# A second weight load moved from the head of a decode kernel to its tail, with two column tiles, and one copy per engine and one semaphore for the output

## The chip, the cores and the metric

The kernel runs on one core of a Trainium2 chip. The metric is the device time of one execution in microseconds. All executions told here were of the fast state; their granted TensorE clock (the share of full speed that the matmul engine was given, 0.50 or 1.00 at any moment), averaged over the span, was 0.775 to 0.789. Each execution has a time and, a little shorter, the span of the profile. The difference is what comes before the first and after the last recorded work; it was 1.76 to 1.94 us in 27 executions of the kernel before.

## The reference, cut to what matters

One decode step for two sequences. Branch A is attention of 16 query heads over a cache of 8 x 32768 keys and values per sequence, and a projection WO (4096 x 448). Branch B is a small MLP, W1 (448 x 1792), GELU, W2 (1792 x 448). A sigmoid gate mixes the two.

```python
g = _sigmoid((x * gate_w).sum(-1, keepdims=True))
a = _A_ref(x, A_k_cache, A_v_cache, A_wq, A_wo)      # softmax(q K^T) V, then @ wo
b = _B_ref(x, B_w1, B_b1, B_w2, B_b2)                # gelu(x @ w1 + b1) @ w2 + b2
return g * a + (1 - g) * b
```

The two caches make 536.9 MB of the 547.4 MB read. W2 is 1.6 MB, WO 3.7 MB.

## The kernel before

One queue loads everything through a ring of three slots of 8.4 MB: WQ, W1 and W2 share the first slot, then come the tiles of K and V, and last WO, in four pieces. The parts that the change touches (cuts marked):

```python
WOP = (0, 14, 26, 30, 32)            # WO's pieces, in chunks of 128 rows
DQ = Dm // 4                         # 112 columns: four column tiles
...
order = [("WQ", 0), ("W12", 0)]      # W1 and W2 together
# ... K and V tiles ...
order += [("V", LASTV), ("WO", 0)]
...
def do_FB():                         # second product of branch B, at the head
    ...
    for fc in range(FC):             # 14 x 4 matmuls, 128x2 stationary, 112 columns moving
        for q in range(4):
            e.matmul(ps_a[32 * q:32 * q + Bn, :], hT_bf[:, fc, :], w2_v[:, fc, q * DQ:(q + 1) * DQ], ...)
...
def FIN(i):                          # projection with WO, piece i: 32 x 4 matmuls in all
    E.wait(f"pW{i}", ("wo", i))
    for c in range(WOP[i], WOP[i + 1]):
        for q in range(4):
            e.matmul(ps_a[32 * q:32 * q + Bn, :], attnT[:, c:Bn * NC:NC], wo_v[...], ...)
...
# PE, at the end: PV of the last V tile, OT (fold over partitions), TT (transpose), FIN
# ACT: two copies of 112 columns to out_sb;  DVE: two more
# SP:
E.wait("dve", "mix")
E.wait("act", "mix")
dma(lambda e: e.dma_start(out[:, 0, :], out_sb), "d_out", "out")
```

FB and FIN add into the same sums in PSUM (`ps_a`), so nothing else joins the branches. Four outputs at partitions 0, 32, 64 and 96 are four column tiles of the PE array, which run at the same time: FIN took 24.7 ns for each matmul of 112 columns, where a score matmul of 512 columns over the whole array took 427 ns at the same half clock, that is 93 ns for 112 columns.

Names used below: PE, DVE, ACT and SP are the matmul, vector, scalar and synchronising engines. S are the score matmuls (q K^T), PV the product of the probabilities with V, HT the first product of branch B (with W1). A transfer has landed when its last semaphore increment has come. The trace calls `ps_a` and `out_sb` by the memory that they lie in, ps_f and pexp.

## Time and profile before

| | kernel before |
|---|---|
| time, median of 4 beside the changed kernel | 1274.07 us (1273.90 to 1274.15) |
| span of the profile | 1272.2 us |
| bytes read | 547.43 MB |
| last piece of V landed | 1259.90 us |
| WO's last piece landed | 1268.53 us |
| FIN ended | 1268.98 us |
| output issued / second landing of the output | 1269.96 / 1271.79 us |

From the page of the kernel before: the busy time of PE, the busy share of the DMA engines in 40 slices of the span (9 is 90% or more), the mean rate, and the chain of work that ended last.

```profile
span 1272.2 us, 8282 instructions
...
PE 693.5 (55%) x4640; PEld 145.3 (11%) x2112; DVE 686.0 (54%) x529; ACT 43.8 (3%) x184; POOL 3.3 (0%) x14
...
DMA  9999999999999999999999999999999999999998
...
HBM read 547.43 MB, written 0.00 MB: 430 GB/s over the span
...
DMA 63%; DVE 20%; PE 14%; issue 3%; SPq 0%; another core or an unknown queue 0%; DVEq 0%
```

The DMA engines are busy for 90% or more of every slice but the last. The Trainium skill, "DMA: Bandwidth & Descriptors", section Specifications, gives 435 GB/s as the ceiling of the fabric; this trace's 430 GB/s agrees. The kernel is bound by its bytes, so a change that removes none can only touch what lies before the stream starts and after it ends.

The end of the timeline (start, duration, engine, line, operation, count, and in brackets how long the engine had been idle and what released it):

```profile
1259.94 1.89 PE L536 MATMUL ps_o<-ring,PT 128*24 128x512 bf16 x16 [3.85 <-DMA ring<-in_A_v_cache_dram]
...
1265.54 0.22 DVE L789 CAST attnT<-ps_m 128x64 bf16<-128x64 f32 x1 [0.77 <-PE ps_m L559]
...
1265.82 3.16 PE L548 MATMUL ps_f<-ring,attnT 128*2 128x112 bf16 x128 [0.32 <-DVE attnT L789]
1269.03 0.50 ACT L653 CAST pexp<-ps_f 2x112 bf16<-2x112 f32 x2 [41.61 <-PE ps_f L548]
1269.03 0.54 DVE L792 CAST pexp<-ps_f 2x112 bf16<-2x112 f32 x2 [3.27 <-PE ps_f L548]
1269.96 0.34 SPq L395 DMA_DIRECT2D out_dram<-pexp  x1
```

Read it as one chain: the last piece of V, its product, the folds on DVE, OT, normalisation, TT, the copy of attnT, and FIN, which runs without a gap from 1265.82 to 1268.98. Then two copies on each of two engines, and the output.

The same stretch by windows (columns: window, its length, busy us and count for PE, weight loads, DVE, ACT, POOL, then the granted PE clock, DMA share and GB/s):

```profile
core 0: us, PE busy (x) PEld busy (x) DVE busy (x) ACT busy (x) POOL busy (x), PEclk, DMA share, GB/s
...
1260.00:1262.00 2.00, 1.84 (x16) 0.38 (x16) 0.11 (x1) 0.00 (x0) 0.00 (x0) 0.50 1.01 427
...
1264.00:1266.00 2.00, 0.78 (x29) 0.69 (x32) 0.91 (x3) 0.00 (x0) 0.00 (x0) 0.50 0.95 389
1266.00:1267.00 1.00, 1.00 (x56) 1.00 (x49) 0.00 (x0) 0.00 (x0) 0.00 (x0) 0.50 0.73 290
1267.00:1268.00 1.00, 1.00 (x56) 1.00 (x48) 0.00 (x0) 0.00 (x0) 0.00 (x0) 0.50 0.42 151
1268.00:1269.00 1.00, 0.97 (x44) 0.66 (x32) 0.00 (x0) 0.00 (x0) 0.00 (x0) 0.50 0.01 2
```

The clock is 0.50 through all of FIN, and the stream is nearly empty from 1268 on (2 GB/s).

At the head (timeline), FB is hidden: it takes 1.48 us, and the first transpose of K comes 10 us later.

```profile
29.92 1.48 PE L455 MATMUL ps_f<-ring,hT_bf 128*2 128x112 bf16 x56 [1.78 <-DVE hT_bf L713]
...
40.20 6.70 DVE L720 STREAM_TRANSPOSE ring<-ring 128x2048 uint32<-128x2048 uint32 x3 [10.33 <-DMA ring<-in_A_k_cache_dram]
```

### The profile page before, as it was taken

To read this page: it belongs to the slowest core of one execution; us is meant where nothing else is said; L and a number is where in the kernel's file an instruction comes from. 1 tells how busy PE (TensorE), PEld (TensorE's weight loads), DVE (VectorE), ACT (ScalarE), POOL (GpSimd) and SP (SyncE) were. 2 spreads that over 40 slices of the span, in tenths; PEclk is the share of its full clock that TensorE was granted. 3 is DMA by queue.
4 is the path that set the end of the run, shared out by engine and by line. 5 is a ranking of instruction groups with operands and counts; after the bars stand their busy time and mean duration, and the time that the engine had idled before them with its cause. 6 is when DMAs were issued, how large, how long until landed. Compare 5 with 4: busy or idle time off the path is not lost.

```text
span 1272.2 us, 8282 instructions
## 1 busy us (share of the span) xinstructions
PE 693.5 (55%) x4640; PEld 145.3 (11%) x2112; DVE 686.0 (54%) x529; ACT 43.8 (3%) x184; POOL 3.3 (0%) x14
## 2 busy tenths in 40 slices
PE   4566566545566444765445655445664546654465
PEld 3111111100111000111001111001110001110011
DVE  2675546745376553655635567353665536556351
ACT  1000000000000000000000000000000000000000
POOL 1000000000000000000000000000000000000000
PEclk9978887777887677877778877788877788867786
DMA  9999999999999999999999999999999999999998
GB/s 409 429 433 429 437 441 427 433 427 441 431 437 435 429 431 433 439 431 437 435 429 431 439 433 431 439 433 429 431 441 431 435 437 431 431 433 439 431 423 353
DMA packets 10973, 547.62 MB, mean 430 GB/s; under 512 B 1352, under 2 KB 1616, under 8 KB 1872
## 3 DMA queue, kind: packets, MB, share of 16 engines
q1 hardware_dynamic: 10804, 547.43, 99.6%
q8 instruction: 9, 0.15, 0.0%
q14 instruction: 4, 0.03, 0.0%
q10 hardware_dynamic: 156, 0.01, 0.0%
HBM read 547.43 MB, written 0.00 MB: 430 GB/s over the span
## 4 chain that ended last, share of the span: by engine, by line
DMA 63%; DVE 20%; PE 14%; issue 3%; SPq 0%; another core or an unknown queue 0%; DVEq 0%
DMA ring<-in_A_k_cache_dram 60%; DVE ring L720 18%; PE ps_s L487 4%; PE ps_s L334 4%; PE ps_o L334 3%; DMA ring<-in_A_v_cache_dram 3%; DVE mx L724 1%; PE ps_o L536 1%; PE ps_m L496 0%; PE ps_m L501 0%; DVE gmax L726 0%; PE ps_f L548 0%; DVE gmx L730 0%; SPq L376 0%
## 5 line engine op out<-in xcount | busy, mean ns | idle before, releaser
L720 DVE STREAM_TRANSPOSE ring<-ring 128x2048 uint32<-128x2048 uint32 x256 | 565.2, 2274 | 393.0 <-DMA ring<-in_A_k_cache_dram 392.8
L487 PE MATMUL ps_s<-ring,Abd 128*128 128x512 bf16 x1024 | 426.1, 416 | 429.8 <-DVE ring L720 429.4
L334 PE MATMUL ps_s<-ring,Abd 128*128 128x512 bf16 x1024 | 422.8, 413 | 0.0
L487 PEld LDWEIGHTS ps_s<-ring,Abd 128*128 128x128 bf16 x1024 | 106.0, 104 | 851.5 <-DVE ring L720 483.5
L334 PE MATMUL ps_o<-ring,PT 128*24 128x512 bf16 x1504 | 111.9, 404 | 0.0
L536 PE MATMUL ps_o<-ring,PT 128*24 128x512 bf16 x544 | 57.1, 418 | 12.8 <-DMA ring<-in_A_v_cache_dram 12.8
L506 PE MATMUL ps_f<-o_sb,selg 128*32 128x257 f32 x32 | 17.0, 636 | 83.4 <-DVE o_sb L761 83.4
L761 DVE SCALAR_TENSOR_TENSOR o_sb<-ps_o,mask,o_sb 128x256 f32<-128x256 f32 x112 | 54.2, 484 | 9.1 <-PE ps_o L536 5.1
L724 DVE TENSOR_REDUCE mx<-ps_s 128x1 f32<-128x1024 f32 x16 | 19.6, 1225 | 60.0 <-PE ps_s L334 60.0
L632 ACT ACTIVATE negm<-ps_m 128x1 f32<-128x1 f32 x16 | 2.7, 171 | 1157.6 <-PE ps_m L501 1157.6
L737 DVE STREAM_TRANSPOSE PT<-pexp 128x1024 bf16<-128x1024 bf16 x16 | 19.9, 1244 | 36.8 <-PE ps_o L334 36.8
L536 PEld LDWEIGHTS ps_o<-ring,PT 128*24 128x24 bf16 x544 | 14.6, 98 | 102.3 <-issue 85.3
L734 DVE COPY ls<-lsum 128x1 f32<-128x1 f32 x16 | 2.5, 154 | 31.8 <-ACT pexp L636 31.8
L626 ACT COPY Abd<-qrep 32x16 bf16 (+1 forms) x128 | 19.4, 199 | 0.6
L636 ACT ACTIVATE pexp<-ps_s,negm 128x1024 bf16<-128x1024 f32 x16 | 17.8, 1113 | 1.7
L496 PE MATMUL ps_m<-ident_f,mx 128*1 128x128 f32 x32 | 6.1, 270 | 21.1 <-DVE mx L724 21.1
L758 DVE TENSOR_SCALAR o_sb<-ps_o,mask 128x256 f32<-128x256 f32 x16 | 7.6, 475 | 15.7 <-PE ps_o L334 15.7
L506 PEld LDWEIGHTS ps_f<-o_sb,selg 128*32 128x32 f32 x32 | 2.9, 141 | 101.5 <-DVE o_sb L761 101.5
L501 PE MATMUL ps_m<-ones_f,gmx 1*128 1x1 f32 x32 | 6.0, 256 | 9.9 <-DVE gmx L730 9.9
L726 DVE TENSOR_REDUCE gmax<-ps_m 1x2 f32<-1x128 f32 x16 | 4.5, 278 | 7.5 <-PE ps_m L496 7.5
L419 PE MATMUL ps_s<-xT,ring 128*128 128x2 bf16 x128 | 3.6, 165 | 8.2 <-DMA ring<-in_A_wq_dram 8.2
L501 PEld LDWEIGHTS ps_m<-ones_f,gmx 1*128 1x128 f32 x32 | 4.7, 183 | 14.6 <-DVE gmx L730 14.6
(76 smaller groups left out, 61.5 us busy)
## 6 DMA issues: line engine op xcount, KB each, us to landing
ring<-in_A_v_cache_dram SPq DMA_DIRECT2D x1, 4096.0 KB, 26.8
ring<-in_A_v_cache_dram SPq DMA_DIRECT2D x2, 2048.0 KB, 33.5
ring<-in_A_wq_dram SPq DMA_DIRECT2D x1, 3072.0 KB, 10.6
ring<-in_B_w_dram SPq DMA_DIRECT2D x1, 1568.0 KB, 17.9
ring<-in_A_wo_dram SPq DMA_DIRECT2D x1, 1568.0 KB, 32.4
ring<-in_B_w_dram SPq DMA_DIRECT2D x1, 1344.0 KB, 13.7
ring<-in_A_wo_dram SPq DMA_DIRECT2D x1, 1344.0 KB, 35.3
ring<-in_A_wq_dram SPq DMA_DIRECT2D x1, 512.0 KB, 11.4
```

Of the source, the lines that this page charges most:

```text
L334: return e.add_instruction(mybir.InstMatmult(name=f"I-{nc.next_id()}", engine=mybir.EngineType.PE, ldweights=False, ins=[e.lower_ap(x), e. ...
L487: fn = lambda e, o=o, x=x, st=st, sp=sp, s=s, w=w: e.matmul(o, a_win(s, w), x, start=st, stop=sp, skip_group_check=True)
L501: E.ins(lambda e: e.matmul(ps_m[:, C_BC:C_BC + 1], gmx[:, :], ones_f[0:1, 0:1], start=True, stop=True), key=("M2", g))
L506: E.ins(lambda e: e.matmul(ps_oa, selg[:, :], o_sb[:, :], start=False, stop=False, skip_group_check=True), key=("OT", g))
L536: fn = lambda e, o=o, x=x, wt=wt, st=st, sp=sp, j=j: e.matmul(o, wt, x, start=st, stop=sp, skip_group_check=True)
L626: E.ins(lambda e, o=o, Q=Q, c=c: e.copy(o[:, :, c:c + 2], qrep[32 * Q:32 * Q + 32, :, bass.ds(E.dyn(2 * g, 2), 2)]), key=(("A", g) if (Q = ...
L636: E.ins(lambda e: e.activation(pexp[:, :].rearrange("p (r i a) -> p i r a", r=CR, i=2), ps_s[:, :].rearrange("p (i r a) -> p i r a", i=2, ...
L720: E.ins(lambda e: e.transpose(k_words(idx, blk), k_words(idx, blk)), key=("T", idx, blk))
L724: E.ins(lambda e: e.tensor_reduce(mx[:, :], ps_s[:, :], AX.X, ALU.max), key=("MX", g))
L737: E.ins(lambda e: e.transpose(PT[:, :], pexp[:, :]), key=("PT", g))
L758: E.ins(lambda e, p=p, m=m: e.tensor_scalar(o_sb[:, 0:Dh], p, m, None, op0=ALU.mult), key=("OS0", g))
L761: E.ins(lambda e, p=p, m=m: e.scalar_tensor_tensor(out=o_sb[:, 0:Dh], in0=p, scalar=m, in1=o_sb[:, 0:Dh], op0=ALU.mult, op1=ALU.add), key= ...
```

## The change

Intent: take W2 out of the head, so that K, V and the chain behind the last V piece come earlier by W2's transfer, and fill the PE's idle time in the tail with FB. Halve the number of matmuls in FB and FIN by two tiles of 224 columns. Shorten the last step to one copy on each of two engines and a single semaphore. WO's four pieces also become 16, 12, 3 and 1 chunks instead of 14, 12, 4 and 2, and the product with b2 stays at the head. The core of the diff:

```diff
-    WOP = (0, 14, 26, 30, 32)
-    DQ = Dm // 4
+    WOP = (0, 16, 28, 31, 32)
+    DQ = Dm // 2
...
-        order = [("WQ", 0), ("W12", 0)]
+        order = [("WQ", 0), ("W1", 0)]
...
-        order += [("V", LASTV), ("WO", 0)]
+        order += [("V", LASTV), ("W2", 0), ("WO", 0)]
...
-            E.wait("dve", "mix")
-            E.wait("act", "mix")
+            E.wait_total("mix")
...
-                    for q in range(4):
+                    for q in range(2):
                         E.ins(lambda e, c=c, q=q: e.matmul(
-                            ps_a[32 * q:32 * q + Bn, :], attnT[:, c:Bn * NC:NC],
+                            ps_a[64 * q:64 * q + Bn, :], attnT[:, c:Bn * NC:NC],
... (the same in FB and in the product with b2)
             OT(NG - 1)
             TT()
+            do_FB()
             E.wait("dve", "at")
...
-            for q in (2, 3):
-                E.ins(lambda e, q=q: e.copy(out_sb[:, q * DQ:(q + 1) * DQ], ps_a[32 * q:32 * q + Bn, :]),
-                      key=("mix" if q == 3 else None))
+            E.ins(lambda e: e.copy(out_sb[:, DQ:Dm], ps_a[64:64 + Bn, :]), key="mixa", stream="mix")
... (the same on DVE with tensor_copy)
```

More of the change, by code (lines that the diff above doesn't have):

```diff
@@ L190, in bass_gated_mix__gqa_block_cached__dense_activation_gelu__decode_kernel @@
         sch.stream(nm, 1)
+    sch.stream("mix", 1)
     for i in range(NB):
@@ L196, in bass_gated_mix__gqa_block_cached__dense_activation_gelu__decode_kernel @@
         sch.stream(f"pW{i}", 16)
-    for nm in ("d_w12", "d_x", "d_gw", "d_b", "d_out"):
+    for nm in ("d_w1", "d_w2", "d_x", "d_gw", "d_b", "d_out"):
         sch.stream(nm, 16)
@@ L269, in kv_src @@
             return cache[b, kvh, t * P * R:(t + 1) * P * R, :].rearrange("(p r) d -> p (r d)", p=P)
-        W_WQ, W_W12 = KC * HD + HW, KC * Fd + HF + FC * Dm
-        assert W_WQ + W_W12 <= SLOT
+        W_WQ, W_W1 = KC * HD + HW, KC * Fd + HF
+        assert W_WQ + W_W1 <= SLOT and (NC + FC) * Dm <= SLOT
         LASTV = NTILES - 1
-        order = [("WQ", 0), ("W12", 0)]
+        order = [("WQ", 0), ("W1", 0)]
         for i in range(NTILES + LAG):
@@ L279, in bass_gated_mix__gqa_block_cached__dense_activation_gelu__decode_kernel @@
                 order.append(("V", i - LAG))
-        order += [("V", LASTV), ("WO", 0)]
-        slot_of = {("WQ", 0): 0, ("W12", 0): 0}
+        order += [("V", LASTV), ("W2", 0), ("WO", 0)]
+        slot_of = {("WQ", 0): 0, ("W1", 0): 0}
         rot = [d for d in order if d[0] in "KV" and d != ("V", LASTV)]
@@ L285, in bass_gated_mix__gqa_block_cached__dense_activation_gelu__decode_kernel @@
         s_wo = slot_of[("V", LASTV - 2)]
-        slot_of[("WO", 0)] = s_wo
+        slot_of[("WO", 0)] = slot_of[("W2", 0)] = s_wo
         slot_of[("V", LASTV)] = slot_of[("K", NTILES - 1)]
@@ L291, in bass_gated_mix__gqa_block_cached__dense_activation_gelu__decode_kernel @@
             s = slot_of[d]
-            if d == ("W12", 0):
+            if d in (("W1", 0), ("WO", 0)):
                 before_of[d] = []
@@ L303, in released @@
             kind, idx = d
-            return {"K": ("S", idx, NCK // 2 - 1), "V": ("PV", idx), "WQ": "QT", "W12": "FB"}[kind]
+            return {"K": ("S", idx, NCK // 2 - 1), "V": ("PV", idx), "WQ": "QT", "W1": "HT"}[kind]
         cut = lambda s, lo, n: ring[:, s * SLOT + lo:s * SLOT + lo + n]
@@ L310, in bass_gated_mix__gqa_block_cached__dense_activation_gelu__decode_kernel @@
         w1_v = w1_f.rearrange("p (k n) -> p k n", k=KC)
-        w2_f = cut(0, W_WQ + KC * Fd + HF, FC * Dm)
+        w2_f = cut(s_wo, NC * Dm, FC * Dm)
         w2_v = w2_f.rearrange("p (f n) -> p f n", f=FC)
@@ L370, in prog_sp @@
                         dma(lambda e, o=o, src=src: e.dma_start(o, src), "slot0", ("wq", i))
-                elif kind == "W12":
+                elif kind == "W1":
                     parts = [(w1_f, B_w1[0:KC * P, :].rearrange("(p k) n -> p (k n)", p=P)),
-                             (w1_r, B_w1[KC * P:Dm, :].rearrange("p (h n) -> (p h) n", h=2)),
-                             (w2_f, B_w2.rearrange("(p f) n -> p (f n)", p=P))]
+                             (w1_r, B_w1[KC * P:Dm, :].rearrange("p (h n) -> (p h) n", h=2))]
                     for i, (o, src) in enumerate(parts):
-                        dma(lambda e, o=o, src=src: e.dma_start(o, src), "d_w12", ("w12", i))
+                        dma(lambda e, o=o, src=src: e.dma_start(o, src), "d_w1", ("w1", i))
+                elif kind == "W2":
+                    dma(lambda e: e.dma_start(w2_f, B_w2.rearrange("(p f) n -> p (f n)", p=P)), "d_w2", "w2")
                 elif kind == "WO":
@@ L433, in do_HT @@
             def do_HT():
-                E.wait_total("d_w12")
+                E.wait_total("d_w1")
                 E.wait("dve", "omB")
@@ L445, in do_HT, with do_B2 @@
                             key=("HT" if (fc == FC - 1 and hf == 1) else None))
+            def do_B2():
+                E.wait("dve", "b2f")
+                for q in range(2):
+                    E.ins(lambda e, q=q: e.matmul(ps_a[64 * q:64 * q + Bn, :], dg[:, :], b2_f[:, q * DQ:(q + 1) * DQ],
+                                                  start=False, stop=False, skip_group_check=True))
             def do_FB():
-                E.wait("dve", "b2f")
-                for q in range(4):
-                    E.ins(lambda e, q=q: e.matmul(ps_a[32 * q:32 * q + Bn, :], dg[:, :], b2_f[:, q * DQ:(q + 1) * DQ],
-                                                  start=False, stop=False, skip_group_check=True))
                 E.wait("dve", "hT")
+                E.wait_total("d_w2")
                 for fc in range(FC):
-                    for q in range(4):
+                    for q in range(2):
                         E.ins(lambda e, fc=fc, q=q: e.matmul(
-                            ps_a[32 * q:32 * q + Bn, :], hT_bf[:, fc, :], w2_v[:, fc, q * DQ:(q + 1) * DQ],
-                            start=False, stop=False, skip_group_check=True),
-                            key=("FB" if (fc == FC - 1 and q == 3) else None))
+                            ps_a[64 * q:64 * q + Bn, :], hT_bf[:, fc, :], w2_v[:, fc, q * DQ:(q + 1) * DQ],
+                            start=False, stop=False, skip_group_check=True))
             def do_GG():
@@ L546, in FIN @@
                 for c in range(WOP[i], WOP[i + 1]):
-                    for q in range(4):
+                    for q in range(2):
                         E.ins(lambda e, c=c, q=q: e.matmul(
-                            ps_a[32 * q:32 * q + Bn, :], attnT[:, c:Bn * NC:NC],
+                            ps_a[64 * q:64 * q + Bn, :], attnT[:, c:Bn * NC:NC],
                             wo_v[:, c * Dm + q * DQ:c * Dm + (q + 1) * DQ], start=False, stop=(c == NC - 1),
-                            skip_group_check=True), key=("FIN" if (c == NC - 1 and q == 3) else None))
+                            skip_group_check=True), key=("FIN" if (c == NC - 1 and q == 1) else None))
             def TT():
-                E.wait("pool", "ts1")
                 E.wait("dve", "on")
@@ L566, in prog_pe @@
             do_HT()
-            do_FB()
+            do_B2()
             def K(idx):
@@ L587, in prog_pe @@
             PV(LASTV)
+            E.wait("pool", "ts1")
             OT(NG - 1)
             TT()
+            do_FB()
             E.wait("dve", "at")
@@ L790, in prog_dve @@
             E.wait("pe", "FIN")
-            for q in (0, 1):
-                E.ins(lambda e, q=q: e.tensor_copy(out_sb[:, q * DQ:(q + 1) * DQ], ps_a[32 * q:32 * q + Bn, :]),
-                      key=("mix" if q == 1 else None))
+            E.ins(lambda e: e.tensor_copy(out_sb[:, 0:DQ], ps_a[0:Bn, :]), key="mixd", stream="mix")
         progs = {"pool": prog_pool, "sp": prog_sp, "pe": prog_pe, "act": prog_act, "dve": prog_dve}
```

## The prediction

> **What bounds the kernel now.** The page shows 547.4 MB read in a 1272.2 us span, 430 GB/s, with the DMA engines at 9 tenths in every slice but the last; the chain of waits is 63% DMA, PE and DVE are busy 55% and 54%. The Trainium skill, "DMA: Bandwidth & Descriptors" (Specifications), gives a fabric ceiling of 435 GB/s; this trace agrees. The change moves no byte out of the kernel, so only the head and the tail can move.
>
> **Tail before (timeline from 1256 us).** Last V piece 1259.94; last PV 1.9 us; the two DVE folds, OT, normalise, TT and the attnT copy follow; FIN (128 matmuls of 112 columns) runs 1265.82 to 1268.98 without a gap, 24.7 ns each; copies 0.54 us; then the output DMA. The table of stretches shows the DMA nearly empty from 1268.0. So the end is bound by the compute chain behind the last V piece, with WO landing about 1 us ahead of FIN's end.
>
> **What moves.** W2 (1.6 MB) at 425 GB/s is 3.75 us (estimate). K0, and with it every tile to the last V piece, lands 3.75 us earlier: last V piece at about 1256.2, TT done about 1261.8. The stream's end stays at about 1268.0. W2 lands at about 1260, before TT ends, so FB does not wait for it. FB (before: 56 matmuls, 1.48 us at 29.9 us, hidden under the wait for K0) is now in the tail.
>
> **Two column tiles.** PV shows four column tiles overlapping: in the cold state 12 matmuls of 512 columns take about 1.3 us net, 107 ns each, a quarter of the 427 ns pitch of the full-array score matmuls. The clock in the tail before is 0.50 from 1256.7 on. 224 columns at half clock are about 187 ns, over two tiles 93 ns a matmul, against 4 x 112 columns at 23.3 (measured 24.7). So at half clock FB costs 28 x 93 = 2.6 us and FIN 64 x 93 = 6.0 us instead of 3.16: half the instructions, twice the streaming time. Warm, 1.3 and 3.0 us.
>
> **Sum (estimate).** FB 1261.8 to 1264.4, when WO's first piece (16 of 32) lands, 1264.2. If the clock stays at half, FIN ends at about 1270.4, 1.4 us later than before. If continuous work releases it (Trainium skill, "TensorE: Matmul & The Clock Gate", Part 1: about 3.4 us of sustained work; PV here went warm 2.6 to 3.1 us after its bursts began at 1240.4 and 1250.2), FIN follows WO's landings and ends 1268.4 to 1269.1. I am not sure that this thin work counts: 6.7 us of dense two-column HT matmuls at the head did not warm it (the score matmuls at 44.8 us are still cold). One copy of 224 columns in place of two of 112 saves about 0.16 us on each of ACT and DVE; the single semaphore little. Weighted: +0.4 minus 0.2, about +0.2 us. I predict 1274.3 us, 1273.0 to 1275.6; faster by over 2%: 0.005, within 2%: 0.985, slower: 0.01.
>
> **What would show it.** K0's first transpose at about 36.5 instead of 40.20 us; last V piece near 1256.2; W2 landed before FB starts; FB plus FIN near 8.6 us of PE time at clock 0.50, or near 5 with a switch to 1.00; the end of DMA unchanged near 1268; one copy near 0.37 us.
>
> **What would make it wrong.** Two column tiles not overlapping (FIN 12 us, +6); the stream pausing at the tail because slot releases moved; WO's smaller last pieces landing late; a clock switch early enough to leave only the DMA end (-1 us).

## More of the kernel before

The waits of the issuing engine at the end, from the list of waits of SP: for the copies, then for its last transfer.

```profile
SPq L100 <- ACT pexp L653: 36.5, 1, 36.5
SPq L804 <- DMA out_dram<-pexp: 1.5, 1, 1.5
```

The first line is a wait instruction of its own (L100, for ACT), which ended at 1269.57 us; the output was issued 0.39 us after that.

## The result, and the profile after

| | before | changed | changed, repeated later |
|---|---|---|---|
| time, median | 1274.07 us | 1273.61 us | 1272.96 us (before beside it: 1274.08) |
| range of the executions | 1273.90 to 1274.15 (4) | 1273.17 to 1274.27 (4) | 1272.78 to 1274.02 (5) |
| ratio to before, 95% interval | | 0.9997 (0.998 to 1.0014) | 0.9994 (0.998 to 1.0007) |
| spans | 1272.2 (profile) | 1271.2 to 1271.8 | 1270.8 to 1271.3 |
| time outside the span | 1.76 to 1.94 (27) | 1.87 to 2.67 | 1.89 to 2.82 |

A ratio is the mean time of one kernel's runs over the mean of the other's in the same rounds, so it is not quite the ratio of the medians that are quoted. The intervals contain 1. What is argued below is about 1 us in 1274, less than such an interval resolves; it rests on ranges of executions, and the text says where they overlap, and on positions in the profiles. The changed kernel's ranges overlap with those of the kernel before, 1273.90 to 1274.15 in the first comparison and 1273.82 to 1274.43 in the second.

The page of the changed kernel:

```profile
span 1271.6 us, 8088 instructions
...
PE 698.9 (55%) x4544; PEld 146.0 (11%) x2016; DVE 685.8 (54%) x528; ACT 43.7 (3%) x183; POOL 3.3 (0%) x14
...
DMA 63%; DVE 21%; PE 13%; issue 3%; SPq 0%; another core or an unknown queue 0%
```

Its timeline at the end:

```profile
1256.61 1.89 PE L539 MATMUL ps_o<-ring,PT 128*24 128x512 bf16 x16 [3.00 <-DMA ring<-in_A_v_cache_dram]
...
1262.09 2.78 PE L459 MATMUL ps_f<-ring,hT_bf 128*2 128x224 bf16 x28
...
1264.76 2.14 PE L551 MATMUL ps_f<-ring,attnT 128*2 128x224 bf16 x32
...
1267.90 1.70 PE L551 MATMUL ps_f<-ring,attnT 128*2 128x224 bf16 x32 [1.00 <-DMA ring<-in_A_wo_dram]
1269.64 0.34 ACT L656 CAST pexp<-ps_f 2x224 bf16<-2x224 f32 x1 [45.75 <-PE ps_f L551]
1269.64 0.38 DVE L793 CAST pexp<-ps_f 2x224 bf16<-2x224 f32 x1 [7.21 <-PE ps_f L551]
1270.05 0.33 SPq L396 DMA_DIRECT2D out_dram<-pexp  x1
```

The product of the last V piece starts 3.33 us earlier (1256.61 for 1259.94), FB takes 2.78 us in the tail, and FIN now waits: 1.00 us, for WO. Two single copies of 0.34 and 0.38 us replace two pairs, and the output is issued 0.03 us after the copies (1269.64 + 0.38 = 1270.02).

By windows (columns as before):

```profile
1264.00:1266.00 2.00, 2.00 (x28) 1.29 (x26) 0.00 (x0) 0.00 (x0) 0.00 (x0) 0.58 0.96 401
1266.00:1267.00 1.00, 0.90 (x20) 0.59 (x14) 0.00 (x0) 0.00 (x0) 0.00 (x0) 1.00 0.73 287
1267.00:1268.00 1.00, 0.10 (x4) 0.10 (x6) 0.00 (x0) 0.00 (x0) 0.00 (x0) 1.00 0.33 122
1268.00:1269.00 1.00, 1.00 (x24) 0.93 (x22) 0.00 (x0) 0.00 (x0) 0.00 (x0) 1.00 0.04 13
```

The clock was half until 1265.7 us and full after that, so FIN's first half is partly slow and its second half fast: 32 matmuls of 224 columns in 1.70 us.

At the head, the first transpose of K comes 3.76 us earlier:

```profile
36.44 11.09 DVE L722 STREAM_TRANSPOSE ring<-ring 128x2048 uint32<-128x2048 uint32 x5 [8.96 <-DMA ring<-in_A_k_cache_dram]
```

And SP's waits at the end. The copies are now waited for by the issuing instruction itself (L396), and the wait for the output is 0.8 us for 1.5:

```profile
SPq L396 <- DVE pexp L793: 41.8, 1, 41.8
SPq L804 <- DMA out_dram<-pexp: 0.8, 1, 0.8
```

The DMA stream's end can be told from the trace's semaphore increments, one from each of the 16 DMA engines that carry WO's last piece (microseconds; this table is worked out from the records, not a view of the page):

```
                      first    mean     last
before               1266.48  1267.57  1268.53
changed              1266.16  1267.57  1268.97
changed, repeated    1266.38  1267.50  1268.35
```

The mean is the same to 0.01 us in the first two and 0.07 us earlier in the third: the stream ends when its bytes are through. What differs from one execution to another is how far the 16 engines spread, 2.0 to 2.8 us here.

### The profile page after: what moved, and what is told of

Same layout as the page of the kernel before. It is cut to its first block, busy times and chain, and to the rows that moved or that the text cites. A ratio compares the mean times of both kernels' runs of the same rounds, so it can differ in the third digit from the quotient of the medians.

```text
span 1271.6 us, 8088 instructions
## 1 busy us (share of the span) xinstructions
PE 698.9 (55%) x4544; PEld 146.0 (11%) x2016; DVE 685.8 (54%) x528; ACT 43.7 (3%) x183; POOL 3.3 (0%) x14
## 4 chain that ended last, share of the span: by engine, by line
DMA 63%; DVE 21%; PE 13%; issue 3%; SPq 0%; another core or an unknown queue 0%
DMA ring<-in_A_k_cache_dram 60%; DVE ring L722 19%; PE ps_o L335 4%; PE ps_s L490 3%; PE ps_s L335 3%; DMA ring<-in_A_wo_dram 3%; DVE mx L726 1%; PE ps_o L539 1%; PE ps_m L499 0%; PE ps_m L504 0%; DVE gmax L728 0%; DVE gmx L732 0%; PE ps_f L551 0%; SPq L376 0%
```

## The experiments

Each run had five rounds beside the kernel before. "Span" is the median of the five spans; the span of the kernel before had medians of 1272.4, 1272.0 and 1272.3 us on the three chips that were used. Two theories stood at the start. Theory 1: the move of W2 pays for what two column tiles cost, and what remains of the gain comes from the last step. Theory 2: the move is the gain, and the tiles cost nothing. The first four runs shared a chip.

### W2 at the head again

The changed kernel, with this undone:

```diff
-        order = [("WQ", 0), ("W1", 0)]
+        order = [("WQ", 0), ("W1", 0), ("W2", 0)]
...
-        order += [("V", LASTV), ("W2", 0), ("WO", 0)]
+        order += [("V", LASTV), ("WO", 0)]
...
             do_B2()
+            do_FB()
```

Expected: 

> The changed kernel with W2 loaded again behind W1 at the head and its product computed there; two column tiles, one copy per engine, one semaphore and the new pieces of WO stay. Theory 1 (the move pays for the two tiles): FIN starts near 1265.8 us in the profile as in the kernel before, and its 64 matmuls take 93 ns each at half clock (6.0 us), less if the clock is released on the way (never under 3.0 us), so it ends at 1269.5 to 1271.8 and the kernel takes about 1275.0 us (1274.2 to 1276.2), slower than the changed kernel. Theory 2 (the two tiles cost nothing, the move itself is the gain): FIN takes about 3.2 us and the time is that of the kernel before less its last step, 1273.6 to 1274.1.

Measured: 1275.08 us (1274.29 to 1275.63), span 1273.1; before 1274.23 (1273.71 to 1274.98). From its timeline:

```profile
1265.80 5.71 PE L552 MATMUL ps_f<-ring,attnT 128*2 128x224 bf16 x64 [0.32 <-DVE attnT L792]
...
1271.55 0.38 DVE L794 CAST pexp<-ps_f 2x224 bf16<-2x224 f32 x1 [5.81 <-PE ps_f L552]
```

FIN starts where it started before, takes 5.71 us for the same arithmetic that took 3.16 with four tiles, and ends 2.5 us later than before. 5.71 us over 64 is 89 ns a matmul, the last 0.6 us of it at full clock; half-clock streaming of 224 columns over two tiles was estimated at 93. So two column tiles do cost their streaming time where FIN is on the chain. Theory 2 falls in this half. The range lies wholly above the changed kernel's (1273.17 to 1274.27): with two tiles, the move is worth 1.5 us in the median (the two were not run side by side).

### The move alone

The kernel before with W2's load and FB moved; four tiles, the old pieces, two copies per engine, two waits.

Expected: 

> The kernel before with only the move of W2 and of its product; four column tiles, the old pieces of WO, two copies per engine and two waits stay. Theory 1: FB takes about 1.45 us in the tail, FIN follows the landings of WO and ends about 0.2 us after the last one instead of 0.45 us, so 1273.8 to 1274.1 us: the move alone gains 0 to 0.3 us, because WO's last landing does not move. Theory 2: the whole gain or more, 1273.2 to 1273.6.

Measured: 1275.05 us (1274.12 to 1275.33), span 1273.3. Both theories missed: the move alone loses about 0.8 us in the median, though the ranges overlap (before 1273.71 to 1274.98). The profile is of the slowest of the five. Timeline, and the landings of WO's last two pieces (line, size, microseconds from issue to landing):

```profile
1269.71 0.36 PE L551 MATMUL ps_f<-ring,attnT 128*2 128x112 bf16 x8 [1.40 <-DMA ring<-in_A_wo_dram]
...
1270.12 0.54 DVE L796 CAST pexp<-ps_f 2x112 bf16<-2x112 f32 x2 [8.19 <-PE ps_f L551]
1271.06 0.34 SPq L396 DMA_DIRECT2D out_dram<-pexp  x1
```

```profile
ring<-in_A_wo_dram SPq DMA_DIRECT2D x1, 448.0 KB, 41.1
ring<-in_A_wo_dram SPq DMA_DIRECT2D x1, 224.0 KB, 42.3
```

FIN's last 8 matmuls waited 1.40 us for the last piece, which landed at 1269.67, 1.8 us after the piece before it, though it is only 224 KB. Of the 16 engines, fifteen had landed it by 1268.46, one at 1269.67. The trace also has a 16 KB instruction fetch that started at 1267.14 and took 1.10 us on its DMA engine. The Trainium skill, "Runtime: NRT & Kernel Launch", section Instruction fetch mechanics, says that each engine's instructions are refilled in 16 KiB blocks over a DMA queue of its own, and calls the cost mostly hidden. The packet's size agrees. In this execution a fetch beside the last packets of the stream, with the delay of one engine that fits it, was not hidden: 1.2 us on the landing that FIN waits for. That the fetch is on the delayed engine is inferred from size and time; the records do not name the DMA engine. The packets fit: the last eight of 1792 bytes, one engine's share of the piece, start at 1268.23, as the fetch ends (1268.24), and run one after another to 1269.25. A fetch there need not cost this much: in five other traces one started at 1267.4 to 1267.6, and the last landing was 0.0 to 0.5 us behind the fifteenth. Nor is it the only cause of a late engine: in the first profile of the changed kernel, which has no fetch there, the last was 0.64 us behind.

### One semaphore alone

The kernel before, with only this:

```diff
-            E.wait("dve", "mix")
-            E.wait("act", "mix")
+            E.wait_total("mix")          # both engines increment one semaphore; wait for 2
```

Expected: 

> The kernel before with only the last two waits merged into one semaphore. Theory 1: the output DMA issues 0.02 to 0.05 us after the last copy instead of 0.39 us, and the time falls by 0.3 to 0.4 us, to about 1273.7. Theory 2: no change, 1274.0 to 1274.15.

Measured: 1273.04 us (1272.87 to 1273.24), span 1271.2; before 1273.71 to 1274.98, no overlap. That is 1.2 us in the median, three times what theory 1 said. Timeline and wait:

```profile
1269.12 0.54 DVE L792 CAST pexp<-ps_f 2x112 bf16<-2x112 f32 x2 [3.26 <-PE ps_f L548]
1269.69 0.33 SPq L395 DMA_DIRECT2D out_dram<-pexp  x1
```

```profile
SPq L804 <- DMA out_dram<-pexp: 0.8, 1, 0.8
```

The issue comes 0.03 us after the copies, as expected (0.36 us gained). The rest is in the landing: the wait for the output falls from 1.5 to 0.8 us. The output's two rows are two packets, each with a landing of its own; before, the second landed 0.67 us after the first, here 0.01 us.

### Four tiles in the changed kernel

`DQ = Dm // 4` and four matmuls per chunk again, so two copies per engine; all else as changed.

Expected: 

> The changed kernel with four column tiles of 112 columns again (and so two copies per engine, still one semaphore). Theory 1: FB 1.45 us instead of 2.8, FIN 24.7 ns a matmul whatever the clock is, so the executions spread over 0.3 us or less instead of the 1.1 us of the changed kernel; the median is 1273.4 to 1273.9, since the part of FIN behind WO's second piece (64 matmuls, 1.6 us) is as long as 32 warm ones of 224 columns (1.7 us). Theory 2: as the changed kernel in median and in spread.

Measured: 1273.23 us, but the five lie in two groups: 1273.04, 1273.09, 1273.23 and 1274.25, 1274.48. The spread that was expected to shrink to 0.3 us is 1.4 us. In the profile (of a fast one) FB took 1.48 and FIN's second half 1.66 us, as expected; a 16 KB fetch stands at 1267.54 and delayed none of the landings. So the spread of executions is not the clock's effect on two tiles.

### The clock kept released

The changed kernel with 15 added 128x512 matmuls in the waits of the tail (3 and 7 ahead of the second and third piece of V, 3 before OT, 2 before TT). This run and the next three shared a second chip.

Expected: 

> The changed kernel with 15 added matmuls of 128x512 into a free part of PSUM, in the waits between the last pieces of V, before the fold product and before the transpose products, so that the TensorE clock stays released in the tail. If the clock is the rest of what the two column tiles cost: clock 1.00 from about 1257 us to the end, FB about 1.4 us instead of 2.8, FIN behind WO's second piece 1.7 us as in the profile of the changed kernel, and since every execution is now like its fast ones, a median of 1273.1 to 1273.4 with a spread under 0.5 us. If the spread of the changed kernel comes from elsewhere (which instruction fetch falls where among the DMA packets), the median stays within 0.2 us of 1273.6 and the spread near 1 us.

Measured: 1273.42 us (1272.99 to 1274.44), span 1271.5. Timeline:

```profile
1260.93 1.51 PE L459 MATMUL ps_f<-ring,hT_bf 128*2 128x224 bf16 x28
...
1267.38 1.70 PE L559 MATMUL ps_f<-ring,attnT 128*2 128x224 bf16 x32 [1.44 <-DMA ring<-in_A_wo_dram]
```

The clock was 1.00 from 1260.5 us on, and FB took 1.51 us instead of 2.78. Nothing came of it: FIN's second half waited 1.44 us for WO instead. The median lies at the edge of both windows; the spread of 1.45 us decides, so the clock explains neither the spread nor a loss of the changed kernel. The cost of two tiles in FB is real and lies off the critical path.

### The old pieces of WO

`WOP = (0, 14, 26, 30, 32)` in the changed kernel.

Expected: 

> The changed kernel with the pieces of WO of the kernel before (14, 12, 4, 2 of 32 instead of 16, 12, 3, 1). The second wait of FIN then ends about 0.5 us earlier and 12 matmuls instead of 8 stand behind the third piece. FIN should end 0.2 to 0.3 us after the last landing instead of 0.63: 0.2 to 0.4 us faster than the changed kernel, 1273.2 to 1273.5, if the clock is released by then; 0.5 us slower if it is not. If the sizes of the pieces play no part, 1273.6.

Measured: 1272.86 us (1272.81 to 1273.05), span 1270.9; before 1273.94 (1273.76 to 1274.33). FIN ended 0.40 us after the last landing, where the unaltered changed kernel needed 0.63. The expectation of 0.2 to 0.3 was missed by a little, and the time was better than expected. Repeated below beside the changed kernel.

### No W2 at all

The changed kernel without W2's load and FB (wrong: relative error 0.13).

Expected: 

> The changed kernel without the load of W2 and without its product (a wrong result on purpose). If the whole time is the bytes of the stream plus a fixed head and tail, the last landing of WO and the time fall by 1.6 MB at 430 GB/s, 3.7 us: 1269.5 to 1270.1. If W2 in the tail costs more or less than its bytes (because of its place or its product), the time falls by clearly more or less than 3.7 us.

Measured: 1271.45 us (1270.76 to 1272.03), span 1269.5. WO's last landing is at 1264.87 us; in the run with the old pieces it was 1268.54, so the stream ended 3.67 us earlier, as 1.6 MB at 430 GB/s says (3.7). But the time missed the window: it fell by 1.4 us against the run with the old pieces on this chip, 2.2 us against the changed kernel's 1273.61 on another, and 2.5 us against the kernel before:

```profile
1262.13 5.34 PE L551 MATMUL ps_f<-ring,attnT 128*2 128x224 bf16 x64 [0.32 <-DVE attnT L790]
```

With no W2 to wait behind, FIN (5.34 us, at half clock until 1266.5) is again on the chain, and ends 2.6 us after the last landing. The bytes set the stream's end; whether the stream's end is the kernel's end depends on the chain beside it.

### Two waits again in the changed kernel

Two theories of the 0.67 us between the output's landings. F: ACT and DVE, done with their copies, have instructions fetched over the same DMA engines, and with two waits the output comes late enough to stand behind those fetches. W: two waits split the landings by themselves.

Expected: 

> The changed kernel with two waits instead of one semaphore ahead of the output DMA. Theory F (the second wait delays the issue by 0.37 us, and the rest of the 1.2 us that the one semaphore gave the kernel before is one of the two output packets standing behind two 8 KB instruction fetches that come about 1.05 us after the two copies of 112 columns, 1.42 us after one copy of 224): here the output packets still come 0.2 to 0.3 us ahead of the fetch, so the two landings of the output stay within 0.05 us of each other and only 0.3 to 0.45 us are lost: 1273.9 to 1274.1. Theory W (two waits by themselves split the landings by 0.65 us): about 1.0 to 1.2 us are lost, 1274.6 to 1274.8, landings 0.65 us apart.

Measured: 1273.60 us (1273.45 to 1274.31), span 1271.7, below the windows of both theories.

```profile
1269.27 0.38 DVE L793 CAST pexp<-ps_f 2x224 bf16<-2x224 f32 x1 [7.22 <-PE ps_f L551]
1270.04 0.34 SPq L396 DMA_DIRECT2D out_dram<-pexp  x1
```

```profile
SPq L804 <- DMA out_dram<-pexp: 0.9, 1, 0.9
```

The issue is 0.39 us after the copies again, and the output's landings are both at 1271.28, not 0.65 us apart. Theory W falls. F had put the output's packets ahead of the fetch; the first started 0.12 us after one, and they still kept together. Against the two runs of the same chip with one semaphore and otherwise nearly this kernel (spans 1271.5 and 1270.9), the loss is 0.2 to 0.8 us, which does not pin the expected 0.3 to 0.45.

### ACT and DVE end late

The kernel before, two waits and all, with `E.wait_total("d_out")` at the end of ACT's and DVE's programs. This run and the next three shared a third chip.

Expected: 

> The kernel before, two waits and all, but ACT and DVE end only after the output has landed. Theory F (the output's second landing comes 0.67 us after the first because ACT and DVE, done with their copies, have their next instructions fetched through the same DMA engines): the two 8 KB fetches now come after the output, the two landings lie within 0.1 us of each other, and the span falls by 0.5 to 0.7 us to about 1271.5, though the output is still issued 0.39 us after the copies; the time itself falls by less if the later fetch lengthens what follows the span. Theory W (the two waits split the landings): landings still 0.65 us apart, span 1272.0 to 1272.4.

Measured: 1273.86 us (1273.63 to 1274.11), span 1272.0; before 1274.08.

```profile
1268.90 0.54 DVE L793 CAST pexp<-ps_f 2x112 bf16<-2x112 f32 x2 [3.27 <-PE ps_f L548]
1269.83 0.34 SPq L395 DMA_DIRECT2D out_dram<-pexp  x1
```

```profile
SPq L806 <- DMA out_dram<-pexp: 0.9, 1, 0.9
```

The issue is still 0.39 us late, yet the wait for the output is 0.9 us instead of 1.5. The records of the output and of the 8 KB fetches around it, from five traces (starts of packets, then the two landings; us):

```
                         8 KB fetches        output packets      landings
before                 1270.60, 1270.65    1270.71, 1271.07    1271.12, 1271.79
the move alone         1271.70, 1271.76    1271.81, 1272.33    1272.27, 1273.13
one semaphore alone    1270.73, 1271.08    1270.45, 1270.48    1270.84, 1270.85
two waits again        1270.67             1270.79, 1270.83    1271.28, 1271.28
ACT and DVE end late   1270.47             1270.58, 1270.62    1271.08, 1271.08
```

With two fetches just ahead, one output packet starts 0.36 to 0.52 us after the other and lands 0.67 to 0.86 us after it. With one fetch or none ahead, the two keep together. In both traces with two, the second output packet starts just as the later fetch ends: 1271.07 (1270.65 and 0.43 us) and 1272.33 (1271.76 and 0.57 us). That this packet stood behind that fetch is read from these times, since the records do not name DMA engines. Holding back ACT's and DVE's ends removed one of the two fetches from in front of the output and the split with it. Theory F had said that both would come after the output; one did (1272.15 us), so whose the other is stays open. Open too is the rest of the split: the late packet also needed 0.3 us longer from start to landing. The Trainium skill, "DMA: Bandwidth & Descriptors", section Queues, rings and completion order, says that each DMA engine takes turns between the queues that have work for it, a packet at a time; these two starts agree with it. The span fell by 0.3 us, less than the 0.5 to 0.7 expected, because from the last landing to the span's end now took 0.76 us instead of 0.39: ACT and DVE had still to end.

### The changed kernel and the old pieces on one chip

Expected of the changed kernel, unaltered: 

> The changed kernel once more, unaltered, beside the runs below on one chip. 1273.2 to 1273.9 us, span of the profile 1271.2 to 1271.8 us, with perhaps one execution of five near 1274.3 whose extra time lies after the span, as in one of four before.

Expected of the old pieces: 

> The changed kernel with the old pieces of WO again, on the chip of the unaltered changed kernel: 1272.7 to 1273.1 us, 0.4 to 0.8 us faster than the changed kernel. If the first run's advantage was a matter of the chip, no difference.

Measured: changed 1272.96 us (1272.78, 1272.89, 1272.96, 1273.37, 1274.02), a little below the window; old pieces 1272.83 (1272.79 to 1273.01); before 1274.08 (1273.82 to 1274.43). The slowest of the changed kernel's executions has an ordinary span of 1271.2 and 2.82 us outside it. Timeline with the old pieces:

```profile
1264.21 4.70 PE L551 MATMUL ps_f<-ring,attnT 128*2 128x224 bf16 x64
```

The pieces are worth 0.13 us in the median here, not the 0.4 to 0.8 expected from comparing runs of different chips. What the ten executions of the two runs with the old pieces have on nine of the changed kernel is a range of 0.26 us instead of 1.5. This version beats both kernels in the median: 1.25 us, or 0.1%, below the kernel before, with no overlap; the changed kernel's range contains its own.

### Four tiles with the old pieces

Expected: 

> The changed kernel with the old pieces of WO and four column tiles (two copies per engine, one semaphore). The tail then has 56 + 128 matmuls with their weight loads instead of 28 + 64. If the slow executions of the two runs with four tiles and the moved product come from a 16 KB instruction fetch near 1267.1 to 1267.5 us that stands ahead of WO's last packets on one DMA engine: span 1272.2 to 1272.6 in most executions and near 1271.2 in the others, that is two groups about 1.2 us apart, the profile of a slow one showing one landing of WO's last piece over 1 us after the other fifteen. If column tiles matter by their streaming time alone: one group, span 1270.7 to 1271.2, as the same kernel with two tiles.

Measured: 1273.94 us (1273.32 to 1274.66), spans 1271.5, 1272.0, 1272.1, 1272.7, 1272.9. Neither form came: not one narrow group below 1271.2, and not two groups. Its profile is that of the fastest execution, with a 16 KB fetch at 1267.37 and no single late landing. Against two tiles on the same chip (1272.79 to 1273.01) the ranges do not overlap: with W2 in the tail and the old pieces, two tiles are 1.1 us better. That the slow executions lose it to a fetch ahead of WO's last packets, as in the move alone, is argued from that one trace and not shown here.

The medians with one semaphore, side by side (us; old or new pieces of WO marked, copies follow the tiles):

| | four tiles | two tiles |
|---|---|---|
| W2 at the head | 1273.04 (old) | 1275.08 (new) |
| W2 in the tail | 1273.23 (new), 1273.94 (old) | 1273.61 and 1272.96 (new), 1272.86 and 1272.83 (old) |

## Why the prediction was right or wrong

The number was right: 1274.3 predicted, within 1273.0 to 1275.6 and "within 2%", against 1273.61 and later 1272.96, the latter just under the range. The reason is partly not the predicted one, and the sign was wrong: 0.2 us slower was predicted, 0.46 and later 1.12 us faster measured. That the number still fell inside owes something to a range 2.6 us wide.

- **Bytes bound the kernel, and the end of the stream does not move.** Right: WO's landings have the same mean, 1267.57 us, in both first profiles (1267.50 repeated); without W2 they end 3.67 us earlier.
- **Everything to the last V piece comes 3.75 us earlier.** Right: first transpose at 36.44 us (36.5 predicted), last V piece at 1256.57 (1256.2), W2 at 1260.33, ahead of FB at 1262.09.
- **Two tiles double the streaming time.** Right as a cost of PE time: FB 2.78 us (2.6 predicted) and, in the run with W2 at the head, 89 ns a matmul (93 predicted). FB and FIN together took 6.6 us, between the 8.6 and the 5 that were given for half and full clock, because the clock changed at 1265.7, inside FIN. So this thin work does release the clock, which the prediction left open. Its evidence against, the cold score matmuls at 44.8 us, does not show this by itself, since PE had idled for over 13 us before them. But the first clock record in these two traces, at 48.4 and 43.7 us, is a rise during the score matmuls, so as far as the records go the HT products at the head did not release it. Their moving side is 2 columns, that of FB and FIN 224; whether this is the reason was not tested. The Trainium skill, "TensorE: Matmul & The Clock Gate", Part 1, gives about 3.4 us of sustained work; here the clock rose 3.6 us after FB's start, and in the runs without W2 and with W2 at the head 4.4 and 5.1 us after FIN's. Over all seven traces with two tiles in which it rose during this work, that is 3.0 to 5.1 us. The traces show why it varies: the clock records change only on a grid of 3.41 us (they last 3.41, 6.83, 13.65 or 20.48 us), whose place differs from trace to trace, and in each of the seven the clock rose at the end of the first step of the tail in which PE was busy throughout. FIN in the kernel before, 3.16 us long, filled no step.
- **Net of the move and the tiles: +0.4 us.** About right in the first profile, where FIN ended at 1269.60 instead of 1268.98 (+0.6), and 0.0 in the repeated one (1268.98). The two differ by when WO's second piece had landed, 1267.85 and 1267.24 us, which FIN's second half waits for; that half took 1.70 us in both, so the difference is not the clock's. But with W2 in the tail, four tiles were not better than two, once by 1.1 us worse, which the prediction's arithmetic does not contain.
- **One copy saves 0.16 us.** Right: 0.38 for 0.54.
- **"The single semaphore little."** This is the term that was mis-sized. By itself it measured 1.2 us in the median: 0.36 us in the issue of the output, seen in every trace with two waits (0.39 us from copy to issue) against every trace with one (0.03), and about 0.7 us because the output then passes ahead of two instruction fetches, as the table of fetches shows. All four traces with two waits have SP's separate wait instruction, which ends with the copies, and the issue 0.39 us behind it; the ten with one semaphore have none. What SP does in this time the trace does not say. The 0.39 us stood in the profile of before, unread. As one semaphore alone reached 1273.04 us, no gain of the rest of the change is shown.
- **What was gained after the span's end was partly lost.** The changed kernel has 1.9 to 2.1 us outside its span instead of 1.8, and 2.7 and 2.8 us in two of its nine executions; 2.6 us came once in five with two waits again, and nowhere else. The one of these that was profiled has a 16 KB fetch at 1273.53 us, 1.9 us after its span's end; the profiles of the clock kept released and of two waits again have one 1.0 us after theirs, with only 1.9 us outside. Which engine's it is, and why it comes late only sometimes, stays open. So does what makes the executions with four tiles and W2 in the tail spread over 1.3 us.

The sum with measured terms for the first profile: FIN +0.62, copies -0.16, issue -0.36, landing of the output 1.15 us after issue instead of 1.83, -0.68: together -0.6 us, which is the difference of the spans, 1271.6 and 1272.2. The median time fell by 0.46 us.

## What to carry to other kernels

In a kernel bound by its bytes, a load moved within the stream does not move the stream's end. It gains only where the chain behind the other loads is the longer one, as with two tiles here (1.5 us); with four it gained nothing. Look instead at the few steps behind the last landing, and read every gap there, even 0.4 us between a copy and a transfer that waits for it. Here one semaphore that both engines increment was worth more than the rearrangement it came with. Doubling the streaming time of FIN cost 2.5 us where it was on the chain, and that of FB nothing that shows where FIN waited for a transfer, so measure such a piece in its place.

## What the Trainium skill lacked or had wrong

- "Runtime: NRT & Kernel Launch", Instruction fetch mechanics, calls the cost of a 16 KiB refill mostly hidden. In the tails here such a fetch took 1.0 to 1.4 us, and in one trace one of 16 landings came 1.2 us late beside it, though in five others 0.0 to 0.5 us. The page's blocks are 16 KiB; it has nothing on the 8 KB fetches at the end of a program; with two of them ahead of the output, its second landing came 0.67 to 0.86 us after the first.
- No page has the cost of a second wait ahead of a DMA: 0.39 us from the last copy to the issue with two waits, 0.03 us with one.
- "TensorE: Matmul & The Clock Gate", Part 1, does not say whether matmuls with a two-column stationary operand over two column tiles count as activity. They do: the clock rose after 3.0 to 5.1 us of them in seven traces. The HT products at the head, with two columns moving, left no rise in the records.
